# Two heads' last 64 queries in one score tile, in an attention and mixture-of-experts kernel

## The chip, the cores and the metric

The kernel runs on one core of a Trainium2 chip. The metric is the device time of one execution in microseconds (us); lower is better. A core has TensorE (PE; its weight loads are shown as PEld), VectorE (DVE), ScalarE (ACT), GpSimd (POOL), SyncE (SP, here only an issuer of DMAs) and 16 DMA engines. TensorE's clock is granted at one of two levels, 1.2 or 2.4 GHz; the profile gives the granted clock as a share of the higher.

## What is computed

Attention with a threshold, then a dense block, then a routed block. Inputs are float32; the essence of the reference:

```python
# q, k, v: [4, 8, 576, 64]: 4 batches, 8 heads, 576 queries, 64 values a head
scores = scale * q @ k.T
scores = where(scores >= max(scores) - tau, scores, -1e9)
attn = exp(scores - max) / (sum + 1e-9)
x = (attn @ v) as [2304, 512]
x = relu(x @ w_in) ** 2 @ w_out                  # 512 -> 2048 -> 512
# then: tokens with x @ w_skip > 0 go to one of 8 experts (argmax of x @ w_gate):
out = x + gate * (relu(x @ w1[e]) @ w2[e])       # 512 -> 1024 -> 512
```

## The kernel before

The 32 heads are worked on in 16 pairs g = 0, 2, ..., 30 (`pair`). The pairs 0 and 2 are computed in float32 (`pair32`, not changed). The other 14, the 16-bit pairs, split queries and keys into two float16 parts that lie side by side (buffer QK, the keys copied with their halves swapped into K2, named K in the profile), so that two matmuls give a float32-like score. The 576 queries of a head are 4 tiles of 128 and one of 64. `UNITS` groups them as (0, 1), (2, 3) and (4).

One tile is `tile_step`: scores on TensorE into a pair of PSUM banks (S, ps_s in the profile), row maximum and limits on VectorE, the exponential on ScalarE, the mask with the row sum (acc) on VectorE, the float16 high part on ScalarE, and the float16 residue on GpSimd, into a piece of hl. `transpose` then turns a unit (one or two tiles) by a DMA into et0, et1 or et2. `av` multiplies them with the values (v12) into the PSUM bank a, and its sum goes to xo: one `av` for the first 256 queries, one for the other 320. The tiles come in the order: five of head x = 0, five of head x = 1. `finish_pair` inverts the sums (rd), stores them to rd_d, and stores xo to xT_d.

The 2304 tokens are then worked on in nine blocks of 256 (`moe_block`). A block loads its tokens into xr and the stored inverse sums into rb (`ld_scale`), scales them, and splits them into xh and xl. Its 16 steps (`moe_step`) each multiply into a bank (ps_h; in late blocks also ps_t, ps_a), take r = ReLU, hh = r squared on ScalarE, r again as the exact square on VectorE, hlo = r - hh (GpSimd in blocks 0 to 4, VectorE later), and multiply by the second weights into ps_o. The weights of the dense block come in 64-bit form and are decoded by `decode` during attention; the last two units of each kind pass through xr, which no block can use meanwhile. The routed block (`second`) comes after block 8; its weights are loaded and cast from the end of block 8 on (L1484, L1488).

Nothing of the order is written out by hand. Every piece of work is a task of `Flow` with an engine, a cost, and the buffers that it uses; a list scheduler plans all of them, 20 times over, with each task's longest tail in the plan as its priority, and the best plan is issued. Each engine then works off its own list in order. A buffer kind has a count: one et0, et1 and et2, two QK, two K2, three e, two r, two hh, one hlo; three score buffers until pair 6, then two; two banks a until pair 6, then one.

Of the kernel before, what the change touches and what calls it, by code (L numbers as in the profile page):

```python
# [231 lines left out]
P = 128  # L232
# [4 lines left out]
def kernel(  # L237
# [120 lines left out]
    CH = 0  # L358
# [58 lines left out]
    def kind(name, n, gate=None):  # L417
# [22 lines left out]
        "pc": (6, [P, 5], F32),  # L440
        "QK": (2, [P, 2 * NQ, P], F16), "K2": (2, [P, S], F16),
        "e": (3, [P, S], F32),
        "et0": (1, [P, 2, NB, P], F16), "et1": (1, [P, 2, NB, P], F16), "et2": (1, [P, 1, NB, REM], F16),
        "xo": (1, [P, S], F32), "sm": (6, [P, 3], F32),
        "acc": (3, [P, 2, NQ], F32), "rd": (3, [P, 2, NQ], F32),
    }
    for n, (c, shape, dt) in ATT.items():
# [26 lines left out]
    flow.kind("etf", [tuple(chunks(i * NQ * P * 4, NQ * P * 4)) for i in range(NF)])  # L474

    MOE = {
        "r": (2, [P, BLK], F32), "hh": (2, [P, BLK], F32R),
        "hlo": (1, [P, BLK], F32R),
        "lg": (2, [P, TPB, E + 1], F32), "gs": (2, [P, 8, TPB], F32),
        "t1": (2, [P, TPB, E], F32), "t2": (2, [P, TPB, E], F32),  # L480
# [111 lines left out]
    def pair(g, parts):  # L592

        s0 = g * NQ
        f = lambda z: s0 - NQ + z
        nqk, nv, v12, vs, qs, pc, spl = (Buf(n) for n in ("nqk", "nv", "v12", "vs", "qs", "pc", "sp"))
        kl, ql = Buf(), Buf()
        queued(sp, "nqk", s0 - 2 * NQ + 1, 1100, lambda on: load_k(on, nqk.at, g), writes=[kl], alloc=[nqk], ns=1200, any=1)
        sp(s0 - 2 * NQ + 1.1, 600, lambda on: load_q(on, nqk.at, g), writes=[ql], alloc=[nqk], ns=1800, any=1)
        queued(sp, "nv", s0 - NQ - 1, 1100, lambda on: load_v(on, nv.at, g), writes=[nv], ns=1800, any=2)  # L600
        if g == AF:
            def clear():
                for j in (KB, NQ + KB):
                    nc.gpsimd.memset(nqk.at[REM:P, :, j, :], 0.0)

            pool(400, s0 - 2 * NQ + 1, clear, parts=[kl, ql], alloc=[nqk], after=[last["nqk"]])
        ready = split(g, f, nqk, kl, ql, qs, pc, spl)
        values(g, f, nv, v12, vs)
        qks = [keys(x, lambda z: f(z + x * NQ), spl, ready[x]) for x in range(2)]
        for units in parts:  # L610
            xo, acc, rd = (Buf(n) for n in ("xo", "acc", "rd"))
            t0, t1 = UNITS[units[0]][0], UNITS[units[-1]][1]
            for x in range(2):
                et = {}
                for u in units:
                    a, b = UNITS[u]
                    et[u] = Buf(f"et{u}")
                    hl = Buf("hl2" if b - a > 1 else "hl")
                    hs = [tile_step(s0 + i - t0, g, u, i, hl, *qks[x], pc, x, acc) for i in range(a, b)]
                    transpose(s0 + b - 1 - t0, u, hl, hs, et[u])  # L620
                    if u != 1:
                        us = range(max(0, u - 1), u + 1)
                        av(s0 + b - t0, g, x, us, [et[z] for z in us], v12, vs, xo)
                s0 += t1 - t0
            finish_pair(g, t0, t1, acc, rd, xo)

    def pair32(g):
# [43 lines left out]
    def tiles32(g, x, a, b, nv, qk, acc, rd, xq):  # L671
        ps2 = Buf("a0" if g < AE else "a")
        done = []
        for i in range(a, b):
            o, m = QT[i]
            s_ = g * NQ + x * NQ + i
            part = Buf()
            ps, e = tile_step(s_, g, 0, i, None, None, None, None, x, acc, qk, part)
            done.append(part)
            et = Buf("etf")  # L680
            fv = lambda ps=ps: ps.at.rearrange("p a b -> p (a b)")

            def turn(m=m, e=e, fv=fv):
                for t in range(NQ):
                    n = min(P, S - t * P)
                    nc.tensor.transpose(
                        fv()[0:n, t * P:t * P + m], e.at[:m, t * P:t * P + n], idf[0:m, 0:m])

            def move(m=m, et=et, fv=fv):
                for r, t0, t1 in ((P, 0, KB), (REM, KB, NQ)):  # L690
                    nc.scalar.copy(
                        out=et.at[0:r, t0:t1, 0:m],
                        in_=fv()[0:r, 0:NQ * P].rearrange("p (t q) -> p t q", q=P)[:, t0:t1, 0:m])

            def product(m=m, et=et, c=(i - a) * D):
                for t in range(NQ):
                    n = min(P, S - t * P)
                    nc.tensor.matmul(  # L698
                        out=ps2.at[:m, c:c + D], lhsT=et.at[0:n, t, 0:m], rhs=nv.at[0:n, x, t, :],
                        start=t == 0, stop=t == NQ - 1)  # L700

            pe(690 if m == P else 380, s_ + 0.4, turn, reads=[e], writes=[ps], heat=0.5)
            queued(act, "hl", 650, CH + s_ + 0.5, move, reads=[ps], writes=[et])
            queued(pe, "av", AV, s_ + 0.6, product, reads=[et, nv], writes=[ps2], heat=0.5)

        def inverse():
            nc.vector.tensor_scalar(
                out=rd.at[:, x, a:b], in0=acc.at[:, x, a:b], scalar1=1e-9 * ESC, scalar2=None, op0=ALU.add
            )
            nc.vector.reciprocal(out=rd.at[:, x, a:b], in_=rd.at[:, x, a:b])  # L710

        k = min(b, KB)

        def scaled():
            nc.vector.tensor_tensor(
                out=xq.at[:, a:k, x], in0=ps2.at[:, 0:(k - a) * D].rearrange("p (t d) -> p t d", d=D),
                in1=rd.at[:, x, a:k, None].to_broadcast([P, k - a, D]), op=ALU.mult)

        def rest_():
            nc.scalar.activation(  # L720
                out=xq.at[0:REM, KB, x], in_=ps2.at[0:REM, (KB - a) * D:(NQ - a) * D],
                func=ACTF.Copy, scale=rd.at[0:REM, x, KB:NQ])

        r = Buf()
        dve(300, -20, inverse, reads=[acc] + done, writes=[r], alloc=[rd], port=1)
        dve(150 + 68 * (k - a), -20, scaled, reads=[ps2, r], parts=[xq], alloc=[rd])
        if b > KB:
            act(190, -20, rest_, reads=[ps2, r], parts=[xq], alloc=[rd])
# [131 lines left out]
        for z in range(a, b):  # L860
            stores.setdefault(bb * NQ + z, []).extend(ts)

    def tile_step(s, g, u, i, hl, QK, K2, pc, x, acc, qk32=None, done=None):
        o, m = QT[i]
        ps, e, sm = Buf("S3" if g < SE else "S"), Buf("e0" if g < EE else "e"), Buf("sm")
        h = Buf()
        row = i - UNITS[u][0]
# [12 lines left out]
                    out=fv()[:m, c], lhsT=qk32.at[0][r, o:o + m], rhs=qk32.at[1][r, c], start=True, stop=True)  # L880

        def scores():
            qk = QK.at.rearrange("p t d -> p (t d)")
            for c in (slice(0, KB * P), slice(KB * P, S)):
                for src, k0 in ((qk, NQ * P), (K2.at, 0)):
                    nc.tensor.matmul(  # L886
                        out=fv()[:m, c], lhsT=qk[:, o:o + m],
                        rhs=src[:, k0 + c.start:k0 + c.stop], start=k0 > 0, stop=k0 == 0,
                    )

        top = lambda: fv()[:m, S:S + 1]

# [31 lines left out]
        if qk32:  # L924
            queued(pe, "S", 1220, s, scores32, reads=[qk32], writes=[ps], heat=0.5)
        else:
            queued(pe, "S", 530, s, scores, reads=[QK, K2], writes=[ps])
        dve(670, CB + s + 0.1, rowmax, reads=[ps], writes=[sm])
        dve(314, CB + s + 0.11, limits, reads=pcs + [ps], writes=[sm])
        act(718, CB + s + 0.2, expo, reads=pcs + [ps, sm], writes=[e])  # L930
# [4 lines left out]
        pool(1382, CH + s + 0.5, lo, reads=[e], writes=[h], alloc=[hl])  # L935
        return h

    def transpose(s, u, hl, hs, et):
        n = len(hs)
        m = QT[UNITS[u][0]][1]  # L940

        def dma(_):
            nc.sync.dma_start_transpose(
                out=et.at.rearrange("p t n q -> p (t n) q"),
                in_=hl.at[:m].rearrange("p t n -> p (t n)"),
            )

        queued(sp, "et", CH + s + 0.6, 1500 * n if m == P else 750, dma, ns=None, reads=hs, writes=[et], alloc=[hl])

    def av(s, g, x, us, ets, v12, vs, xo):  # L950

        n = [sum(QT[i][1] for i in range(*UNITS[u])) for u in us]
        o = QT[UNITS[us[0]][0]][0]
        ps = Buf("a0" if g < AE else "a")
        top, low = (slice(z * D, z * D + D) for z in (x, 1 - x))

# [2 lines left out]

        def mm():  # L960
            c = 0
            for et, w in zip(ets, n):
                for z in range(NB):
                    vals = v12.at[:, x, z % NQ]
                    for a in range(2) if apart else (slice(0, 2),):
                        lhsT = vals[:, a] if apart else vals.rearrange("p a d -> p (a d)")
                        nc.tensor.matmul(  # L967
                            out=ps.at[0:D if apart else P, c:c + w], lhsT=lhsT, rhs=et.at[:, :, z, :],
                            start=z == 0 and a != 1, stop=z == NB - 1 and a != 0,
                        )  # L970
                c += w
# [107 lines left out]
    def moe_block(j):  # L1079
# [22 lines left out]
        for c in range(2):  # L1102
# [3 lines left out]
            y = j * BLK  # L1106
            while y < (j + 1) * BLK:
                bb, o = divmod(y, S)
                n = min(S - o, (j + 1) * BLK - y)
                ks = [z for z in range(2) if not wide_(bb * H + 4 * c + 2 * z)]  # L1110
                if ks:
                    if todo and todo[-1][0] == ks and todo[-1][2] == y - j * BLK:
# [11 lines left out]
            def ld_scale(on, c=c, rb=rb, todo=todo):  # L1124
                for ks, _, _, segs in todo:
                    for z in range(2):
                        for bb, o, n, w in segs:
                            h0 = 4 * c + 2 * ks[0] + z
                            on.dma_start(
                                out=rb.at[z * D:(z + 1) * D, ks[0]:ks[-1] + 1, w:w + n],  # L1130
                                in_=rd_d[bb, h0:h0 + 2 * len(ks) - 1:2, o:o + n][None].to_broadcast([D, len(ks), n]),
                            )
# [693 lines left out]
```

## Time and profile before

| what | value |
|---|---|
| runs | 1065.97 us (median of 3: 1063.48, 1065.97, 1066.58) |
| profiled execution | 1064.44 us, of it 1062.9 us from its first to its last instruction (the span) |
| busy share of the span | PE 84%, DVE 74%, ACT 57%, POOL 39% |
| mean granted clock of TensorE | 0.901 |
| chain of work that ended last, by engine | PE 55%, DVE 17%, DMA 12%, ACT 6% |

The busy shares are means over stages that differ: the 32-bit pairs, then 16-bit pairs alone, then 16-bit pairs with the blocks 0 to 4 between their tiles, then the rest of the blocks, then the routed block. An engine's share says little without its stage. In the rows, times are us unless marked ns, L886 is line 886 of the kernel before, and "128x1 f32<-128x576 f32" reads: 128 partitions by 1 element from 128 partitions by 576.

### The profile page before, as it was taken

To read this page: it belongs to the slowest core of one execution; us is meant where nothing else is said; L and a number is where in the kernel's file an instruction comes from. 1 tells how busy PE (TensorE), PEld (TensorE's weight loads), DVE (VectorE), ACT (ScalarE), POOL (GpSimd) and SP (SyncE) were. 2 spreads that over 40 slices of the span, in tenths; PEclk is the share of its full clock that TensorE was granted. 3 is DMA by queue.
4 is the path that set the end of the run, shared out by engine and by line. 5 is a ranking of instruction groups with operands and counts; after the bars stand their busy time and mean duration, and the time that the engine had idled before them with its cause. 6 is when DMAs were issued, how large, how long until landed. Compare 5 with 4: busy or idle time off the path is not lost.

```text
span 1062.9 us, 16377 instructions
## 1 busy us (share of the span) xinstructions
PE 890.8 (84%) x5272; PEld 706.9 (67%) x5272; DVE 791.5 (74%) x1927; ACT 602.7 (57%) x1033; POOL 416.1 (39%) x546
## 2 busy tenths in 40 slices
PE   6999843527997899897789798999999996889895
PEld 3676621316775786676666677889999975677674
DVE  6999799869886989995898884445454775688771
ACT  5678676757765777674665764212121552757761
POOL 2323356546565677574565763401010011121211
PEclk9995565659998999898899998999999997989998
DMA  6434586999989999899968998612010536778850
GB/s 172 142 108 142 141 181 123 152 148 175 133 163 103 128 187 200 182 118 126 157 150 162 104 154 81 196 41 80 1 41 1 163 119 238 275 269 293 303 208 21
DMA packets 293864, 156.14 MB, mean 147 GB/s; under 512 B 240468, under 2 KB 266580, under 8 KB 293776
## 3 DMA queue, kind: packets, MB, share of 16 engines
q1 hardware_dynamic: 290096, 148.19, 67.0%
q0 software_dynamic: 3680, 6.89, 2.2%
q8 instruction: 42, 0.69, 0.3%
q14 instruction: 46, 0.38, 0.1%
HBM read 89.29 MB, written 17.28 MB: 100 GB/s over the span
## 4 chain that ended last, share of the span: by engine, by line
PE 55%; DVE 17%; DMA 12%; ACT 6%; issue 4%; SPq 3%; POOL 2%; DVEq 0%; ACTq 0%; POOLq 0%
PE ps_h L1166 9%; PE ps_t L1166 6%; PE ps_o L1176 4%; PE ps_o L1178 4%; PE ps_o L1177 4%; PE ps_o L1588 4%; PE ps_s L879 3%; PE ps_a L967 3%; DVE e L909 3%; PE ps_s L886 3%; DVE ps_s L894 3%; DMA K<-QK 3%; PE ps_t L1556 3%; PE ps_h L698 2%; DMA et<-hl 2%
## 5 line engine op out<-in xcount | busy, mean ns | idle before, releaser
L919 POOL TENSOR_TENSOR hl<-e,hl 128x64 f16<-128x64 f32 (+2 forms) x276 | 205.5, 771 | 122.8 <-ACT hl L915 106.3
L1166 PE MATMUL ps_h<-xh,w 128*128 128x256 f32 x720 | 144.6, 298 | 13.0 <-DVE r L1198 8.1
L886 PE MATMUL ps_s<-QK 128*128 128x512 f16 (+1 forms) x280 | 88.9, 322 | 71.3 <-DVE e L909 70.0
L886 PEld LDWEIGHTS <-QK 128*128 128x128 f16 (+1 forms) x560 | 52.6, 109 | 141.3 <-issue 106.3
L906 ACT ACTIVATE e<-ps_s,sm,pc 128x576 f32<-128x576 f32 (+1 forms) x138 | 112.6, 827 | 50.1 <-DVE sm L901 42.3
L1196 ACT ACTIVATE hh<-r 128x256 fp32r<-128x256 f32 x144 | 60.1, 417 | 141.1 <-DVE r L1191 99.5
L909 DVE SCALAR_TENSOR_TENSOR e<-ps_s,sm,e 128x576 f32<-128x576 f32 (+1 forms) x153 | 122.5, 806 | 17.5 <-ACT e L906 16.6
L894 DVE TENSOR_REDUCE ps_s<-ps_s 128x1 f32<-128x576 f32 (+1 forms) x160 | 120.0, 755 | 19.7 <-PE ps_s L886 15.4
L1166 PEld LDWEIGHTS ps_h<-xh,w 128*128 128x128 f32 x720 | 116.7, 197 | 23.9 <-DVE r L1198 15.1
L1176 PE MATMUL ps_o<-w,hh 128*128 128x512 f32 x288 | 120.5, 418 | 0.0
L915 ACT CAST hl<-e 128x576 f16<-128x576 f32 (+1 forms) x138 | 91.9, 669 | 47.3 <-DVE e L909 31.6
L1178 PE MATMUL ps_o<-w,hlo 128*128 128x512 f32 x288 | 114.9, 399 | 3.4 <-DVE hlo L1202 2.2
L1177 PE MATMUL ps_o<-w,hh 128*128 128x512 f32 x288 | 114.4, 397 | 0.0
L1166 PE MATMUL ps_h<-xl,w 128*128 128x256 f32 x360 | 103.6, 288 | 0.5 <-POOL xl L1147 0.4
L1202 POOL TENSOR_TENSOR hlo<-r,hh 128x256 fp32r<-128x256 f32 x80 | 64.3, 804 | 79.8 <-DVE r L1198 39.2
L1488 DVE TENSOR_TENSOR w<-stg,w 128x1024 fp32r<-128x1024 f32 x63 | 75.7, 1220 | 21.5 <-ACT w L1484 20.8
L967 PE MATMUL ps_a<-et,v 128*128 128x256 f16 (+1 forms) x738 | 78.3, 262 | 12.6 <-DVE xo L980 8.6
L1484 ACT CAST w<-stg 128x1024 fp32r<-128x1024 f32 x63 | 65.0, 1049 | 25.8 <-PE ps_o L1588 11.0
L967 PEld LDWEIGHTS <-v 128*128 128x128 f16 x756 | 60.8, 104 | 28.4 <-issue 10.4
L886 PE MATMUL ps_s<-K,QK 128*128 128x512 f16 (+1 forms) x280 | 71.0, 321 | 4.2 <-DMA K<-QK 4.2
L1041 POOL TENSOR_TENSOR w<-tmp,w 128x512 fp32r<-128x512 f32 x28 | 38.8, 1393 | 83.7 <-ACT tmp L1038 69.1
L1166 PEld LDWEIGHTS ps_h<-xl,w 128*128 128x128 f32 x360 | 70.6, 196 | 0.9 <-POOL xl L1147 0.9
(286 smaller groups left out, 2036.7 us busy)
## 6 DMA issues: line engine op xcount, KB each, us to landing
stg<-in_moe_w_dram SPq DMA_DIRECT2D x63, 512.0 KB, 5.2
raw<-in_moe_w_in_dram SPq DMA_DIRECT2D x14, 512.0 KB, 4.4
raw<-in_moe_w_out_dram SPq DMA_DIRECT2D x14, 512.0 KB, 3.6
big<-in_moe_w_dram SPq DMA_DIRECT2D x13, 512.0 KB, 5.2
xr<-in_moe_w_dram SPq DMA_DIRECT2D x12, 512.0 KB, 5.0
xT_d<-xo SPq DMA_DIRECT2D x16, 288.0 KB, 4.7
xr<-xT_d SPq DMA_DIRECT2D x9, 512.0 KB, 4.6
x_d<-big SPq DMA_DIRECT2D x18, 256.0 KB, 4.5
```

Source lines behind the costliest of these rows:

```text
L886: nc.tensor.matmul(out=fv()[:m, c], lhsT=qk[:, o:o + m], rhs=src[:, k0 + c.start:k0 + c.stop], start=k0 > 0, stop=k0 == 0,)
L894: nc.vector.tensor_reduce(out=top(), in_=sv(), axis=AX.X, op=ALU.max)
L906: nc.scalar.activation(out=ev(), in_=sv(), func=ACTF.Exp, bias=col(1), scale=pc.at[:m, 0:1])
L909: nc.vector.scalar_tensor_tensor(out=ev(), in0=sv(), scalar=col(2), in1=ev(), op0=ALU.is_ge, op1=ALU.mult, accum_out=acc.at[:m, x, i:i + 1],)
L915: nc.scalar.copy(out=hl.at[:m, row, 0:S], in_=e.at[:m])
L919: nc.gpsimd.tensor_tensor(out=hl.at[:m, row, w:w + n], in0=e.at[:m, c:c + n], in1=hl.at[:m, row, c:c + n], op=ALU.subtract,)
L967: nc.tensor.matmul(out=ps.at[0:D if apart else P, c:c + w], lhsT=lhsT, rhs=et.at[:, :, z, :], start=z == 0 and a != 1, stop=z == NB - 1 an ...
L1166: nc.tensor.matmul(out=ps.at[:, 0:BLK], lhsT=a[:, kk, :], rhs=b[:, kk, :], start=kk == z == 0, stop=kk == KC - 1 and z == 2,)
L1176: nc.tensor.matmul(out=p, lhsT=hh.at[:, sl], rhs=bh, start=m == 0, stop=False)
L1177: nc.tensor.matmul(out=p, lhsT=hh.at[:, sl], rhs=bl, start=False, stop=False)
L1178: nc.tensor.matmul(out=p, lhsT=hl.at[:, sl], rhs=bh, start=False, stop=m == KF - 1)
L1488: nc.vector if on == "DVE" else nc.gpsimd).tensor_tensor(
```

## The change

The last 64 queries of both heads of a 16-bit pair are put into one tile of 128 rows: the first head's on partitions 0 to 63, the second's on 64 to 127. It is the fifth of the pair's now nine tiles, between four of the first head and four of the second. Its row sums stand in one column of acc, and the two heads' parts are told apart where the inverse sums are read back. et2 has 128 columns where it had 64, and r has one buffer where it had two. The last two changed pieces below belong to `moe_block`: blocks are read in pieces that end at query 512 of a batch, and the pieces behind it are read from the shared column.

```diff
-        "et0": (1, [P, 2, NB, P], F16), "et1": (1, [P, 2, NB, P], F16), "et2": (1, [P, 1, NB, REM], F16),
+        "et0": (1, [P, 2, NB, P], F16), "et1": (1, [P, 2, NB, P], F16), "et2": (1, [P, 1, NB, P], F16),
...
-        "r": (2, [P, BLK], F32), "hh": (2, [P, BLK], F32R),
+        "r": (1, [P, BLK], F32), "hh": (2, [P, BLK], F32R),
...
+            both = Buf("et2")
             for x in range(2):
-                et = {}
-                for u in units:
+                et = []
+                for u in range(2):
                     a, b = UNITS[u]
-                    et[u] = Buf(f"et{u}")
-                    hl = Buf("hl2" if b - a > 1 else "hl")
-                    hs = [tile_step(s0 + i - t0, g, u, i, hl, *qks[x], pc, x, acc) for i in range(a, b)]
-                    transpose(s0 + b - 1 - t0, u, hl, hs, et[u])
-                    if u != 1:
-                        us = range(max(0, u - 1), u + 1)
-                        av(s0 + b - t0, g, x, us, [et[z] for z in us], v12, vs, xo)
-                s0 += t1 - t0
+                    et.append(Buf(f"et{u}"))
+                    hl = Buf("hl2")
+                    hs = [tile_step(s0 + i, g, u, i, hl, [qks[x]], pc, x, acc) for i in range(a, b)]
+                    transpose(s0 + b - 1, hl, hs, et[u])
+                    if not u:
+                        av(s0 + b, g, x, 0, et, None, v12, vs, xo)
+                s0 += KB
+                if not x:
+                    hl = Buf("hl")
+                    hs = [tile_step(s0, g, 2, KB, hl, qks, pc, 0, acc)]
+                    transpose(s0, hl, hs, both)
+                av(s0 + 1 - x, g, x, 1, et, both, v12, vs, xo)
+                s0 += 1 - x
...
         def scores():
+            for z, (QK, K2) in enumerate(qks):
+                qk = QK.at.rearrange("p t d -> p (t d)")
+                for c in (slice(0, KB * P), slice(KB * P, S)):
+                    for src, k0 in ((qk, NQ * P), (K2.at, 0)):
+                        nc.tensor.matmul(
+                            out=fv()[z * w:z * w + w, c], lhsT=qk[:, o:o + w],
+                            rhs=src[:, k0 + c.start:k0 + c.stop], start=k0 > 0, stop=k0 == 0,
+                        )
...
     def ld_scale (moe_block):
-                n = min(S - o, (j + 1) * BLK - y)
+                n = min((KB * P if o < KB * P else S) - o, (j + 1) * BLK - y)
...
                             h0 = 4 * c + 2 * ks[0] + z
+                            if o >= KB * P:
+                                h0, o = h0 - z, o + z * REM
```

`av` now takes its last 64 columns from the part of et2 that is its head's. The plan is made anew, so rows move on every engine; three places follow, with the buffers' numbers as the program gives them.

TensorE, from the fourth tile of the first head on, in pair 4, where 16-bit work begins (QK_188 and K_193 are the first head's, QK_189 and K_194 the second's; the weight loads between are left out). Before:

```order
L886 MATMUL ps_s_144<-K_193,QK_188 128x64
...
L886 MATMUL ps_s_148<-QK_188 64x512
...
L886 MATMUL ps_s_148<-K_193,QK_188 64x512
...
L886 MATMUL ps_s_148<-QK_188 64x64
...
L886 MATMUL ps_s_148<-K_193,QK_188 64x64
...
L886 MATMUL ps_s_140<-QK_189 128x512
```

Now:

```order
L897 MATMUL ps_s_144<-K_193,QK_188 128x64
...
L897 MATMUL ps_s_140<-QK_188 64x512
...
L897 MATMUL ps_s_140<-K_193,QK_188 64x512
...
L897 MATMUL ps_s_140<-K_193,QK_188 64x64
...
L897 MATMUL ps_s_140<-QK_189 64x512
...
L897 MATMUL ps_s_140<-K_194,QK_189 64x512
...
L897 MATMUL ps_s_140<-K_194,QK_189 64x64
...
L897 MATMUL ps_s_148<-QK_189 128x512
```

The second head's keys are read one tile sooner, into the same score buffer as the first head's last queries.

VectorE, where the first step of block 0 (r_253) stands among the tiles of the 16-bit pairs (ps_s is a row maximum, sm the limits, e the mask, xo an output; xr_249 by big is the block's scaling). Before, at row 443 of VectorE's list and on:

```order
L901 TENSOR_SCALAR sm_224<-ps_s_140,pc_182 128x1
L909 SCALAR_TENSOR_TENSOR e_200,acc_231<-ps_s_144,sm_223,e_200 128x576
L909 SCALAR_TENSOR_TENSOR e_198,acc_231<-ps_s_140,sm_224,e_198 128x576
L583 CAST qs_174<-qs_174 128x2
L894 TENSOR_REDUCE ps_s_144<-ps_s_144 128x1
L1198 SCALAR_TENSOR_TENSOR r_253<-ps_h_136,r_253 128x256
L894 TENSOR_REDUCE ps_s_140<-ps_s_140 64x1
```

Now, at row 412 and on:

```order
L920 SCALAR_TENSOR_TENSOR e_199,acc_230<-ps_s_144,sm_223,e_199 128x576
L920 SCALAR_TENSOR_TENSOR e_198,acc_230<-ps_s_140,sm_224,e_198 128x576
L1205 TENSOR_SCALAR r_253<-ps_h_136 128x256
L849 TENSOR_SCALAR acc_230<-acc_230 128x10
L861 RECIPROCAL rd_236<-acc_230 128x10
L1212 SCALAR_TENSOR_TENSOR r_253<-ps_h_136,r_253 128x256
L905 TENSOR_REDUCE ps_s_144<-ps_s_144 128x1
```

The step stood at row 448, after 54 row maxima of the whole kernel; it now stands at row 417, after 47.

SP's queue, around the load of block 0's tokens (xr_249 from xT_d) and the decode's loads into the same buffer (from in_moe_w_in and in_moe_w_out). Before:

```order
L1012 DMA xr_249<-in_moe_w_in_dram 128x4x256
L943 DMA_TRANSPOSE et_208<-hl 128x18x128
L943 DMA_TRANSPOSE et_212<-hl 128x9x64
L849 DMA rd_d<-rd_237 128x10x1
L849 DMA rd_d<-rd_235 128x10x1
...
L1012 DMA xr_249<-in_moe_w_out_dram 128x1024
...
L1093 DMA xr_249<-xT_d 128x4x256
L1129 DMA big<-rd_d 64x2x256 x2
```

Now:

```order
L1024 DMA xr_249<-in_moe_w_in_dram 128x4x256
L855 DMA rd_d<-rd_237 128x10x1
L855 DMA rd_d<-rd_235 128x10x1
...
L1105 DMA xr_249<-xT_d 128x4x256
L1143 DMA big<-rd_d 64x2x256 x2
...
L953 DMA_TRANSPOSE et_212<-hl 128x9x128
...
L1024 DMA xr_249<-in_moe_w_out_dram 128x1024
```

The fourth of the decode's loads through xr stood ahead of the block's tokens and now stands behind them.

## Rows read from the trace of the kernel before

**Rows 1.** Windows by stage: us, busy time (x instructions) per engine, granted clock, DMA.

```profile
core 0: us, PE busy (x) PEld busy (x) DVE busy (x) ACT busy (x) POOL busy (x), PEclk, DMA share, GB/s
...
120.00:250.00 130.00, 58.53 (x319) 33.87 (x318) 111.54 (x267) 87.92 (x139) 70.15 (x87) 0.62 0.84 147
250.00:660.00 410.00, 360.83 (x2480) 285.20 (x2481) 337.86 (x952) 269.87 (x496) 251.16 (x344) 0.95 0.95 144
660.00:850.00 190.00, 187.90 (x1240) 168.59 (x1239) 97.45 (x257) 47.08 (x107) 24.66 (x35) 1.00 0.26 74
```

**Rows 2.** Lines by form, a tile's chain: busy us, mean ns, idle before.

```profile
L894 DVE TENSOR_REDUCE ps_s<-ps_s 128x1 f32<-128x576 f32 x128 | 96.1, 756 | 15.9 <-PE ps_s L886 12.4 <-PE ps_s L879 2.7
...
L919 POOL TENSOR_TENSOR hl<-e,hl 64x512 f16<-64x512 f32 x28 | 33.1, 1182 | 0.0
...
L909 DVE SCALAR_TENSOR_TENSOR e<-ps_s,sm,e 64x576 f32<-64x576 f32 x31 | 24.9, 804 | 4.2 <-ACT e L906 4.0
...
L894 DVE TENSOR_REDUCE ps_s<-ps_s 64x1 f32<-64x576 f32 x32 | 24.0, 751 | 3.8 <-PE ps_s L886 3.0 <-issue 0.3
...
L906 ACT ACTIVATE e<-ps_s,sm,pc 64x576 f32<-64x576 f32 x28 | 23.0, 822 | 10.2 <-DVE sm L901 9.5 <-POOL hl L919 0.5
...
L915 ACT CAST hl<-e 64x576 f16<-64x576 f32 x28 | 18.7, 666 | 6.1 <-DVE e L909 5.8
...
L897 DVE TENSOR_SCALAR sm<-ps_s,pc 64x1 f32<-64x1 f32 x28 | 7.3, 262 | 0.2
...
L901 DVE TENSOR_SCALAR sm<-ps_s,pc 64x1 f32<-64x1 f32 x28 | 5.6, 199 | 0.0
```

**Rows 3.** TensorE's waits, 250 to 660 us: us in total, times, longest.

```profile
PE ps_s L886 <- DVE e L909: 9.6, 11, 3.0
...
PE ps_s L886 <- DMA K<-QK: 4.2, 3, 2.9
```

**Rows 4.** Lines by form, a score matmul of a whole and of a 64-query tile.

```profile
L886 PE MATMUL ps_s<-QK 128*128 128x512 f16 x112 | 48.6, 434 | 54.3 <-DVE e L909 53.2 <-ACT xo L745 0.6
...
L886 PE MATMUL ps_s<-QK 128*64 128x512 f16 x28 | 12.6, 448 | 17.0 <-DVE e L909 16.8
```

**Rows 5.** Timeline of DVE, SP and PE, 226 to 245 us: start, us.

```profile
226.99 0.49 DVE L1015 TENSOR_SCALAR big<-xr 128x512 int32<-128x512 int32 x1 [7.41 <-DMA xr<-in_moe_w_out_dram]
...
234.94 0.37 SPq L1093 DMA_DIRECT2D xr<-xT_d  x1
...
244.08 0.48 PE L1166 MATMUL ps_h<-xh,w 128*128 128x256 f32 x2
```

**Rows 6.** Timeline around r: third stage, mixed stage, a cast in block 8.

```profile
753.18 0.42 DVE L1191 TENSOR_SCALAR r<-ps_h 128x256 f32<-128x256 f32 x1 [0.90 <-PE ps_h L1166]
...
754.69 0.42 DVE L1202 TENSOR_TENSOR hlo<-r,hh 128x256 fp32r<-128x256 f32 x1
756.00 0.42 DVE L1191 TENSOR_SCALAR r<-ps_a 128x256 f32<-128x256 f32 x1 [0.89 <-PE ps_a L1166]
...
411.57 0.37 ACT L1189 ACTIVATE r<-ps_h 128x256 f32<-128x256 f32 x1
412.16 1.31 POOL L1202 TENSOR_TENSOR hlo<-r,hh 128x256 fp32r<-128x256 f32 x1
...
847.53 1.21 DVE L1488 TENSOR_TENSOR w<-stg,w 128x1024 fp32r<-128x1024 f32 x1
```

**Rows 7.** Timeline of SP and PE, 548 to 557 us, pair 26.

```profile
548.17 1.18 SPq L763 DMA_DIRECT2D K<-QK  x2
...
552.13 0.40 PE L886 MATMUL ps_s<-QK 128*64 128x512 f16 x1
...
552.62 0.20 PE L886 MATMUL ps_s<-K,QK 128*64 128x64 f16 x1
556.20 0.38 PE L886 MATMUL ps_s<-QK 128*128 128x512 f16 x1 [0.36 <-DVE e L909]
```

**Rows 8.** DMA issues: count, KB each, median us to landing.

```profile
K<-QK SPq DMA_DIRECT2D x14, 72.0 KB, 4.3
...
oT<-rd_d SPq DMA_DIRECT2D x4, 32.0 KB, 3.6
```

More of the change, by code (lines that the diff above doesn't have):

```diff
@@ L677, in tiles32 @@
             part = Buf()
-            ps, e = tile_step(s_, g, 0, i, None, None, None, None, x, acc, qk, part)
+            ps, e = tile_step(s_, g, 0, i, None, None, None, x, acc, qk, part)
             done.append(part)
@@ L861, in finish_pair, with tile_step @@
             stores.setdefault(bb * NQ + z, []).extend(ts)
-    def tile_step(s, g, u, i, hl, QK, K2, pc, x, acc, qk32=None, done=None):
+    def tile_step(s, g, u, i, hl, qks, pc, x, acc, qk32=None, done=None):
         o, m = QT[i]
+        w = m
+        if not qk32:
+            m = P
         ps, e, sm = Buf("S3" if g < SE else "S"), Buf("e0" if g < EE else "e"), Buf("sm")
@@ L882, in scores @@
         def scores():
[L883 to L889, printed above, removed]
+            for z, (QK, K2) in enumerate(qks):
[6 more added lines that the diff above has]
+                        )
         top = lambda: fv()[:m, S:S + 1]
@@ L926, in tile_step @@
         else:
-            queued(pe, "S", 530, s, scores, reads=[QK, K2], writes=[ps])
+            queued(pe, "S", 530 * len(qks), s, scores, reads=[z for qk in qks for z in qk], writes=[ps])
         dve(670, CB + s + 0.1, rowmax, reads=[ps], writes=[sm])
@@ L936, in tile_step, with transpose @@
         return h
-    def transpose(s, u, hl, hs, et):
+    def transpose(s, hl, hs, et):
         n = len(hs)
-        m = QT[UNITS[u][0]][1]
         def dma(_):
@@ L944, in dma, with av @@
                 out=et.at.rearrange("p t n q -> p (t n) q"),
-                in_=hl.at[:m].rearrange("p t n -> p (t n)"),
+                in_=hl.at.rearrange("p t n -> p (t n)"),
             )
[L948 to L953, printed above, removed]
+        queued(sp, "et", CH + s + 0.6, 1500 * n, dma, ns=None, reads=hs, writes=[et], alloc=[hl])
+    def av(s, g, x, u, ets, both, v12, vs, xo):
+        n = [2 * P] + [REM] * (both is not None)
+        o = u * 2 * P
+        cuts = [(ets[u], slice(0, P))] + ([(both, slice(x * REM, x * REM + REM))] if both else [])
+        ets = [z for z, _ in cuts]
         ps = Buf("a0" if g < AE else "a")
@@ L961, in mm @@
             c = 0
-            for et, w in zip(ets, n):
+            for (et, q), w in zip(cuts, n):
                 for z in range(NB):
@@ L967, in mm @@
                         nc.tensor.matmul(
-                            out=ps.at[0:D if apart else P, c:c + w], lhsT=lhsT, rhs=et.at[:, :, z, :],
+                            out=ps.at[0:D if apart else P, c:c + w], lhsT=lhsT, rhs=et.at[:, :, z, q],
                             start=z == 0 and a != 1, stop=z == NB - 1 and a != 0,
```

## The prediction

> **What bounds the kernel now.** I read the share of busy time by stage first [rows 1]. There are four stages behind the 32-bit pairs (0 to 120 us, untouched by the change). From 120 to 250 us three 16-bit pairs run while the weights are decoded, and no mixture-of-experts block has begun: VectorE is busy 111.5 of 130 us, TensorE 58.5, at a granted clock of 0.62. From 250 to 660 us the other eleven pairs run with blocks 0 to 4 between them: TensorE 360.8 of 410 us, VectorE 337.9, ScalarE 269.9, GpSimd 251.2. From 660 to 850 us TensorE alone counts, 187.9 of 190 us. The last stage has nothing of the change in it. So the first of these stages is set by VectorE, the second mostly by TensorE with VectorE close behind, the third by TensorE. TensorE's work stays what it is, so the end moves by what TensorE's idle time (71.5 us, then 49.2 us) gains or loses.
>
> Then I looked at one tile by its forms [rows 2]. What the reader is to see: a tile of 64 queries costs as much as one of 128, since time goes by the 576 columns. The row maximum takes 751 ns on 64 partitions and 756 ns on 128. Last come the waits of TensorE in the mixed stage [rows 3]: the longest is 9.6 us in all, for a score bank that the mask (L909) still holds. TensorE's idle time there has many small causes.
>
> **The change, part by part.** *Tiles merged.* Each of 14 pairs has nine elementwise chains where it had ten. A chain of the 64-query form is, on VectorE, 751 + 262 + 199 + 804 = 2016 ns; on ScalarE 822 + 666 = 1488 ns; on GpSimd 1182 ns for the long half of the residue and a short second part [rows 2]. Over 14 pairs that is 28.2 us of VectorE and 20.8 us of ScalarE. Two transposing DMAs become one of twice the rows; their bytes are the same.
>
> *TensorE.* The shared tile has the same eight matmuls as two 64-query tiles, and the value products have the same count and widths. A half's first matmul takes 448 ns against 434 ns for a full one [rows 4]; I count nothing.
>
> *The stage to 250 us.* The order shows 448 VectorE rows ahead of the first block's r in the kernel before and 417 now. Seven tiles' maxima, limits and masks are no longer ahead of it (three have gone, four now come after it), and the decode of the last weight unit through xr has also moved behind it. Seven chains are 7 x 2.016 = 14.1 us; VectorE is busy 86% of this stage, so 12 us. The block's first matmul stands at 244.08 us, right after its input is loaded into xr (234.94 us), which waited for that fourth decode, and the decode for its load (VectorE idle 7.41 us) [rows 5]. So two causes let the block start earlier; I take 12 us, not their sum, because the load into xr also waits for the slow store of the pair's sums. TensorE is idle 55% of this stage, so 12 us more of it with work is 12 x 0.55 = 6.6 us gained. Bounds: nothing, if xr's load stays as late; 14 us, if TensorE takes up all of it.
>
> *The mixed stage.* Eleven chains are 22.2 us of VectorE's 337.9 (6.6%) and 16.4 of ScalarE's 269.9 (6.1%). If TensorE's 49.2 us of idle time fell in the same share, that would be 3.2 us; if VectorE were the only limit, 22.2 us. The stage is nearer to the first, with TensorE 88% busy, but some of its time runs at a low clock (0.95 in the mean) and comes back with denser work: I take 5 us. Bounds 0 and 22.2.
>
> *One buffer r instead of two.* Now a step's ReLU may start before the subtraction of the step before it has read r; afterwards it can't. In the third stage it already doesn't: one subtraction starts at 754.69 us and lasts 0.42 us, the next ReLU starts at 756.00 [rows 6], 0.89 us of slack in a step of 2.82 us (the distance of two ReLUs there). In the mixed stage there are steps in which it does: a ReLU at 411.57 us, while the earlier step's subtraction on GpSimd runs from 412.16 for 1.31 us [rows 6]. That step would begin 1.9 us later, and the bank of its matmul would come free as much later. At the end of the third stage the casts of the next weights, 1.21 us each [rows 6], stand between the steps on VectorE: ReLU, square, product and subtraction are some 1.9 us with their handoffs, 3.1 us with a cast, against 2.82 us. Sixteen steps of 0.3 us are 5 us. I take a loss of 2 us for all of it; bounds 0 and 12.
>
> *The second head's keys are wanted a tile sooner.* The shared tile stands fifth and multiplies by both heads' keys; the second head's first tile stood sixth. In pair 26 the copy of the keys is issued at 548.17 us, such copies land 4.3 us later (median) [rows 8], so at about 552.5 us; the fifth tile starts at 552.13, the sixth at 556.20 [rows 7]. A slack of 3.7 us becomes a wait of 0.4 us. TensorE takes its rows in order, so block steps and value products behind those scores wait too. The buffers of the first head likewise come free at the fifth tile and are wanted again four tiles later, not five. I take a loss of 1 us; bounds 0 and 14 (1 us a pair).
>
> *The scales.* The rows of 1/sum are now read by 12 more DMAs of 32 KB, in blocks 4, 6 and 8. Such a one lands in 3.6 us [rows 8]. Blocks 6 and 8 lie in the stage where TensorE has 160 us of queued work, so they are covered; for block 4 the cover is the steps of block 3. Nothing, and at worst one landing, 3.6 us.
>
> The sum: -6.6 - 5 + 2 + 1 = -8.6 us, on the profiled execution's 1064.44 us (its span is 1062.9): 1055.8, so 1056 us. That execution lies 1.5 us under the median of the runs shown, 1065.97, which is less than what the terms leave open.
>
> **A rule weighed against the rows.** A score matmul on half the array takes as long as a full one [rows 4], one after the other, and the sum counts it so. The Trainium skill's page TensorEngine Tiling (Array Packing), Tiling Modes, says that the array's tiles work independently and that different ones can load weights and multiply in parallel; the shared tile's two halves write different partitions, so by that rule they could overlap. No row of before has two such halves in a row. Half of the shared tile's matmuls would then vanish: a 64-query tile's four took some 0.7 us (552.13 to 552.82 us [rows 7]), and 14 of them are 9.8 us of TensorE, which would put the end at 1046. I give it 4 in 100.
>
> **The rivals.** *Slower: the single r.* If in the mixed stage a quarter of the 80 steps lose 1 us on TensorE's path (20 us), and the end of the third stage loses 5, the sum is -11.6 + 1 + 25: 1079 us. It decides from 0.14 us a step on 80 steps, where the 11.6 us of gains are gone. For it: the GpSimd subtraction that lasts 1.31 us, behind chains of residues of 1.18 us. Against it: only some ReLUs lead, and the slack in the third stage. 12 in 100. *Slower: the keys.* With 2 us a pair lost (28 us) and r's 2 us, 1064.4 - 11.6 + 30 = 1083; at 1 us a pair it is 1069, the edge. For it: TensorE already waited for such copies in the mixed stage, 4.2 us in all [rows 3]; against: the planner can fill the space with block steps. 8 in 100. *No change:* the block's start stays tied to the store of sums and xr's load, and the mixed stage to TensorE: gains of 1 to 4, losses of as much, 1062 to 1067. 14 in 100. *Much faster:* the mixed stage follows VectorE (22.2) and the start brings 14: 1064.4 - 36 + 3 = 1031; between it and my forecast, say 1040. 10 in 100.
>
> **How the numbers follow.** My forecast (1047 to 1062) has the remaining 52 in 100. About 0.3% of the median, 3.2 us, is what a measurement can tell from no change. Faster: 0.52 + 0.10 + 0.04 = 0.66. Same: 0.14. Slower: 0.20. The range leaves out a tenth at either end: 1040, where the case much faster begins, to 1072, past the edge of the keys' case.
>
> **What would show it.** Right: 140 row maxima of 16-bit pairs become 126, all on 128 partitions; the first block's matmul stands near 232 us; TensorE's idle time up to 660 us falls by some 9 us; the stage of TensorE alone keeps its 2.82 us a step. Wrong: ReLUs that wait for the subtraction of the step before, TensorE rows of the shared tile that wait for the copy of keys, a block start that is still near 244 us, or an attention that ends earlier while its TensorE work is only pushed into the third stage.

## The result, and the profile after

The changed kernel takes 1049.55 us (median of 4 runs, 1047.54 to 1054.27) where the kernel before took 1064.72 beside it on the same chip: 0.987 of it, 95% interval 0.982 to 0.991. On another chip, later, it took 1057.84 (9 runs) against 1067.24: 0.992 [0.990, 0.995]. The profiled execution took 1047.54 us, its span 1046.0. Times are medians of all executions; ratios, here and below, are of means, without the few executions that lie over 1.5% above the fastest of their kernel.

The stages of [rows 1] now, in the columns of those rows:

```profile
120.00:250.00 130.00, 68.50 (x397) 44.46 (x397) 108.04 (x266) 84.95 (x138) 66.81 (x82) 0.71 0.82 159
250.00:660.00 410.00, 356.25 (x2494) 280.67 (x2490) 318.48 (x901) 254.34 (x473) 236.79 (x328) 0.96 0.95 147
660.00:850.00 190.00, 188.87 (x1250) 171.32 (x1249) 104.89 (x266) 48.51 (x105) 23.12 (x32) 1.00 0.25 80
```

In the stage to 250 us TensorE has 10 us more work than before (block 0 starts earlier); from 250 to 660 us it has 4.6 us less and VectorE 19.4 us less. TensorE's idle time in the two stages is 61.5 + 53.8 = 115.3 us, before 120.6. But the stages are cut at fixed times, and the work in them has moved; the accounts below use the whole span.

The chain of a tile, and the score matmuls of a half tile, by form, as in [rows 2] and [rows 4]:

```profile
L920 DVE SCALAR_TENSOR_TENSOR e<-ps_s,sm,e 128x576 f32<-128x576 f32 x134 | 106.5, 810 | 9.4 <-ACT e L917 7.4 <-issue 1.0
L905 DVE TENSOR_REDUCE ps_s<-ps_s 128x1 f32<-128x576 f32 x142 | 105.8, 757 | 21.9 <-PE ps_s L897 15.3 <-PE ps_s L889 5.8
...
L897 PE MATMUL ps_s<-K,QK 128*64 128x512 f16 x28 | 7.0, 435 | 3.8 <-DMA K<-QK 3.8
L897 PE MATMUL ps_s<-QK 128*64 128x512 f16 x28 | 6.5, 441 | 8.4 <-DVE e L920 8.4
```

142 row maxima on 128 partitions are the 16 of the 32-bit pairs and the 126 that were forecast. In the last two rows the reader is to see the two numbers behind the bar: 28 matmuls of 441 ns are busy for 6.5 us only. Before, 28 of 448 ns were busy for 12.6 us [rows 4]. Busy time counts a moment once: now nearly every pair of them lies in the same moment. TensorE's timeline around the shared tile of one pair shows it (start, us; "x2" is two matmuls in one row):

```profile
473.45 0.18 PE L584 MATMUL ps_a<-vs,ones 128*128 128x1 bf16 x1
473.56 0.42 PE L897 MATMUL ps_s<-QK 128*64 128x512 f16 x2
473.80 0.39 PE L897 MATMUL ps_s<-K,QK 128*64 128x512 f16 x2
474.01 0.21 PE L897 MATMUL ps_s<-QK 128*64 128x64 f16 x2
474.04 0.21 PE L897 MATMUL ps_s<-K,QK 128*64 128x64 f16 x2
474.19 0.18 PE L584 MATMUL ps_a<-qs,ones 128*128 128x2 bf16 x1
```

All eight matmuls of the shared tile end 0.69 us after the first begins, the time of the four of a half tile before (552.13 to 552.82 us [rows 7]), and other work of TensorE starts at 474.19. In the program the second head's four stand behind the first head's four.

The load of block 0's tokens, its scaling and the first block matmul, from the timeline [rows 5]:

```profile
225.75 0.51 SPq L1105 DMA_DIRECT2D xr<-xT_d  x1
...
232.19 1.64 DVE L1153 TENSOR_TENSOR xr<-xr,big 128x512 f32<-128x512 f32 x1
...
234.08 0.78 PE L1180 MATMUL ps_h<-xh,w 128*128 128x256 f32 x2
```

TensorE's waits from 250 to 660 us, as in [rows 3]:

```profile
PE ps_h L1180 <- DVE r L1212: 11.0, 16, 2.4
PE ps_s L897 <- DVE e L920: 7.5, 13, 1.7
PE ps_o L1192 <- POOL hlo L1216: 7.0, 4, 3.3
...
PE ps_s L897 <- DMA K<-QK: 5.4, 2, 3.8
```

The wait for the mask has fallen from 9.6 to 7.5 us, the wait for the keys has grown from 4.2 to 5.4, and the longest in all is now one for a step of the blocks (the product r, 11.0 us; 7.9 before). The step of the third stage is what it was: 2.82 us between two ReLUs, the subtraction done well before [rows 6]:

```profile
753.30 0.42 DVE L1205 TENSOR_SCALAR r<-ps_t 128x256 f32<-128x256 f32 x1 [0.90 <-PE ps_t L1180]
...
754.80 0.43 DVE L1216 TENSOR_TENSOR hlo<-r,hh 128x256 fp32r<-128x256 f32 x1
756.12 0.42 DVE L1205 TENSOR_SCALAR r<-ps_t 128x256 f32<-128x256 f32 x1 [0.90 <-PE ps_t L1180]
```

### The profile page after: what moved, and what is told of

Same layout as the page of the kernel before. It is cut to its first block, busy times and chain, and to the rows that moved or that the text cites. A ratio compares the mean times of both kernels' runs of the same rounds, so it can differ in the third digit from the quotient of the medians.

```text
span 1046.0 us, 16199 instructions
## 1 busy us (share of the span) xinstructions
PE 883.7 (84%) x5272; PEld 701.3 (67%) x5272; DVE 763.7 (73%) x1866; ACT 580.0 (55%) x996; POOL 395.4 (38%) x516
## 4 chain that ended last, share of the span: by engine, by line
PE 33%; DVE 14%; issue 13%; DMA 10%; ACT 5%; POOL 4%; SPq 2%; DVEq 0%; POOLq 0%; ACTq 0%
PE ps_h L1180 7%; PE ps_t L1180 5%; PE ps_o L1192 4%; PE ps_o L1190 3%; DMA QK<-sp 3%; PE ps_o L1191 3%; DVE e L920 3%; DVE ps_s L905 3%; PE ps_a L979 3%; PE ps_s L897 2%; PE ps_o L1602 2%; DVE sp L833 1%; POOL hl L930 1%; DMA K<-QK 1%; DVE r L1212 1%
## 5 line engine op out<-in xcount | busy, mean ns | idle before, releaser
L930 POOL TENSOR_TENSOR hl<-e,hl 128x64 f16<-128x64 f32 x246 | 184.7, 778 | 98.5 <-ACT hl L926 94.8
L1192 PE MATMUL ps_o<-w,hlo 128*128 128x512 f32 x288 | 115.3, 400 | 11.3 <-POOL hlo L1216 7.4
L905 DVE TENSOR_REDUCE ps_s<-ps_s 128x1 f32<-128x576 f32 (+1 forms) x146 | 108.8, 756 | 21.9 <-PE ps_s L897 15.3
L917 ACT ACTIVATE e<-ps_s,sm,pc 128x576 f32<-128x576 f32 x123 | 98.8, 827 | 40.4 <-DVE sm L912 33.3
L920 DVE SCALAR_TENSOR_TENSOR e<-ps_s,sm,e 128x576 f32<-128x576 f32 (+1 forms) x138 | 109.7, 809 | 9.5 <-ACT e L917 7.4
L897 PEld LDWEIGHTS <-QK 128*128 128x128 f16 (+1 forms) x560 | 46.4, 107 | 100.8 <-issue 67.1
L897 PE MATMUL ps_s<-QK 128*128 128x64 f16 (+2 forms) x280 | 77.1, 316 | 35.6 <-DVE e L920 31.2
L926 ACT CAST hl<-e 128x576 f16<-128x576 f32 x123 | 80.5, 667 | 23.9 <-DVE e L920 21.0
L1216 POOL TENSOR_TENSOR hlo<-r,hh 128x256 fp32r<-128x256 f32 x80 | 60.8, 760 | 78.0 <-DVE r L1212 52.5
L1192 PEld LDWEIGHTS ps_o<-w,hlo 128*128 128x128 f32 x288 | 54.7, 190 | 30.0 <-POOL hlo L1216 11.7
```

The source lines that it names most:

```text
L897: nc.tensor.matmul(out=fv()[z * w:z * w + w, c], lhsT=qk[:, o:o + w], rhs=src[:, k0 + c.start:k0 + c.stop], start=k0 > 0, stop=k0 == 0,)
L905: nc.vector.tensor_reduce(out=top(), in_=sv(), axis=AX.X, op=ALU.max)
L917: nc.scalar.activation(out=ev(), in_=sv(), func=ACTF.Exp, bias=col(1), scale=pc.at[:m, 0:1])
L920: nc.vector.scalar_tensor_tensor(out=ev(), in0=sv(), scalar=col(2), in1=ev(), op0=ALU.is_ge, op1=ALU.mult, accum_out=acc.at[:m, x, i:i + 1],)
L926: nc.scalar.copy(out=hl.at[:m, row, 0:S], in_=e.at[:m])
L930: nc.gpsimd.tensor_tensor(out=hl.at[:m, row, w:w + n], in0=e.at[:m, c:c + n], in1=hl.at[:m, row, c:c + n], op=ALU.subtract,)
```

## The experiments

Three explanations stood at the start: block 0 begins earlier; VectorE has 14 chains fewer; and the plan, made anew, happens to be better or worse, whatever the change. Each ratio is to the kernel before in runs beside it.

**Parts of the change.** *One buffer r alone:* the kernel before with `"r": (1, ...)`.

> The kernel before with one buffer r instead of two, nothing else (the plan is made anew). If one buffer costs what the prediction took, +2 us (0.2%); if it costs nothing, within 0.3% of the kernel before; if part of the measured gain is the new plan's luck, a move of 5 us or more either way. A ReLU that waits for the subtraction of the step before would show as idle time of TensorE before the next block matmul.

Measured: 1074.04 us, 1.011 [1.007, 1.014]. Its first block matmul stands at 230.75 us, earlier than in the change, and the kernel is slower than before. An early block 0 is thus not enough.

*The order without the shared tile,* with one r:

```diff
-                    hs = [tile_step(s0, g, 2, KB, hl, qks, pc, 0, acc)]
-                    transpose(s0, hl, hs, both)
+                    for z in range(2):
+                        hl = Buf("hl")
+                        hs = [tile_step(s0 + z, g, 2, KB, hl, [qks[z]], pc, z, acc)]
+                        transpose(s0 + z, hl, hs, each[z], REM)
```

> The new order without the merging: two tiles of 64 queries stand side by side in the place of the shared tile, each with its own chain of maximum, exponential, mask and casts and its own transposing DMA. One buffer r. If the removed chains are the gain, it is gone: within 0.5% of the kernel before, or slower by up to 10 us since the second head's keys are wanted a tile sooner with nothing saved. If the order itself (output products and buffers) were the gain, -8 us or more.

Measured: 1086.65 us, 1.023 [1.020, 1.027]. It is the slowest of all, though nothing in it is wider or longer than in before_r1 (et2 has two buffers of 64 columns there); the change itself, with the tiles in the same place but merged, is 3 to 4% faster. That difference holds three things at once: the chains, the shared matmuls and the plan. Its TensorE waits for copies of the keys before score matmuls are 1.6 us in all, so its loss isn't the keys; its first block matmul stands at 268.66 us, 24.6 us later than in the kernel before. Its timeline of TensorE holds the best comparison for the shared tile, the same eight matmuls, but with both halves on rows 0 to 63 of two banks:

```profile
347.96 0.40 PE L900 MATMUL ps_s<-QK 128*64 128x512 f16 x1
348.20 0.38 PE L900 MATMUL ps_s<-K,QK 128*64 128x512 f16 x1
348.42 0.19 PE L900 MATMUL ps_s<-QK 128*64 128x64 f16 x1
348.45 0.20 PE L900 MATMUL ps_s<-K,QK 128*64 128x64 f16 x1
348.48 0.38 PE L900 MATMUL ps_s<-QK 128*64 128x512 f16 x1
348.70 0.38 PE L900 MATMUL ps_s<-K,QK 128*64 128x512 f16 x1
348.91 0.19 PE L900 MATMUL ps_s<-QK 128*64 128x64 f16 x1
348.94 0.20 PE L900 MATMUL ps_s<-K,QK 128*64 128x64 f16 x1
```

One after the other: 347.96 to 349.14, that is 1.18 us against 0.69 in the shared tile.

*The shared tile in some pairs only* (one r): `JOIN = lambda g: g < 12` for the first four 16-bit pairs, `g >= 12` for the last ten; the others as before.

> Shared tile in the pairs 4 to 10 alone (10 is the pair in which block 0 begins); the pairs 12 to 30 keep two 64-query tiles. One buffer r. Theory A (the gain is made before block 0 and carried to the end): most of the 15 us, some -11 to -15 us. Theory B (each merged pair gives the same, about 1.1 us): 4/14 of it, -4 us.

> Shared tile in the pairs 12 to 30 alone; the pairs 4 to 10 keep two 64-query tiles. One buffer r. Theory A: 0 to -3 us, as in the stretch with blocks, which got 2.3 us shorter. Theory B: 10/14 of the gain, -11 us.

Measured: 1061.99 us, 1.001 [0.998, 1.004], and 1072.65 us, 1.011 [1.008, 1.014]. Ten of 14 merged pairs are slower than four. No gain by pair explains that (theory A isn't borne out either: -11 to -15 us were expected of the four); it made the plan the suspect.

**The plan's own scatter.** In before and in the change, the cost by which the planner counts a mask is 736 instead of 730. The work is the same, the order is another.

```diff
-        dve(730, CB + s + 0.3, mask, ...
+        dve(736, CB + s + 0.3, mask, ...
```

> The kernel before, with the planner told that a mask takes 736 ns and not 730; the same instructions, in another plan. If a plan made anew moves the time little, within 0.3%; if the gain of 15 us can be a plan's luck, a move of 5 us or more.

> The changed kernel with the same nudge of the planner. In this plan all four decodes through xr stand before block 0, whose first r stands at VectorE's row 435 (417 in the change, 448 before). If the gain is the removed work, -12 to -17 us against the kernel before. If it is the early start of block 0 that this one plan found, some -5 us.

Measured: before 1066.09 us, 0.999 [0.995, 1.002]; the change 1064.27 us, 0.997 [0.993, 1.000]. The same change in another order takes 0.4 to 1.0% longer than the change's own order (0.992 and 0.987 on two chips).

**The start of block 0.** In the change, block 0's load is put behind the whole decode (`if j <= 1` for `if j == 1`); in before, the decode's last load through xr is put behind block 0's load.

> The changed kernel with one dependency more: block 0's tokens are loaded into xr only behind the whole decode, as they stood in the kernel before. Theory of the start (block 0 ahead of the fourth decode is what gave the 10 us): -3 to -8 us against the kernel before, block 0 near 244 us. Theory of the removed work: -12 us or more.

> The kernel before with block 0's tokens loaded into xr ahead of the last decode, as in the change, and no tile merged. Theory of the start: -5 to -10 us, block 0 near 234 us. Theory of the removed work: within 0.3%, since VectorE has as much to do ahead of the block (first r at row 446 against 448).

Measured: 1073.59 us, 1.006 [1.003, 1.009], and 1081.47 us, 1.012 [1.007, 1.018]. In the first, the order at xr is the one that was asked for (the fourth decode's load at 213.99 us, the tokens' at 228.18; in the change 247.12 and 225.75), but it didn't delay the block: the new plan decodes sooner, the first block matmul stands at 234.66 us as in the change (234.08), and the kernel is 1.4 to 1.9% slower than the change, whose ratios are 0.992 and 0.987. In the second it moved 3.4 us ahead (240.67), and the kernel is slower. Over all these kernels (the table below has every start) the time doesn't follow this start where it lies between 223 and 245 us. order_only, slowest and latest with 268.66 us, may have lost by its delay; no run tells.

**The single r again, and more plans.** `r1_order_r2` is before_r1 in exactly its order, but the steps take two r in turn. `r1_nudge` is before_r1, and `after_nudge2` the change, with a mask cost of 736 and 724; `after_again` is the change.

```diff
+        rt = place["r"][len(turns) % 2]
...
-                nc.scalar.activation(out=r.at, in_=ps.at[:, 0:BLK], func=ACTF.Relu)
+                nc.scalar.activation(out=rt, in_=ps.at[:, 0:BLK], func=ACTF.Relu)
```

> The kernel before with one r (before_r1, 1.011 of before) in exactly its order of instructions, but each step's r now lies in the other of two buffers, so that a ReLU need not wait for the subtraction of the step before it. Nothing else differs from before_r1. Theory that the waits for the one r cost the time: the 11 us come back, 0.995 to 1.002 of before, and the TensorE waits whose other end is r (12.9 us by the dense block's first matmul between 250 and 650 us) shrink. Rival, that the order which the planner makes with one r costs it: 1.008 to 1.013 still, about 1074 us on a chip where before takes 1063. Half and half: 1.004 to 1.007.

> before_r1 (two r become one, tiles not merged) with the planner's cost of a mask 736 instead of 730, so another plan of the same work. If one r costs 1 percent by itself: 1.007 to 1.015 of before. If before_r1 was an unlucky plan: 0.998 to 1.005. With it, after and its two other plans have as many plans of the unmerged kernel beside them.

> The change itself on the chip of these runs, so that its other plans can be read beside it: 0.983 to 0.991 of before if what was measured first belongs to the kernel and not to the chip; nearer to 0.995 if the first measurement flattered it.

> The change with the planner's cost of a mask 724 instead of 730: another plan of the same work. The nudge to 736 gave 0.9965 of before, the change itself 0.987. If the change's worth lies near the middle of its plans: 0.987 to 0.997. If the change's own plan is the typical one and the nudge to 736 an unlucky one: 0.984 to 0.990. If the change's own plan is a lucky one: 0.994 to 1.000.

Measured, in that order: 1078.61 us, 1.009 [1.006, 1.013]; 1064.15 us, 0.998 [0.994, 1.001]; 1057.84 us, 0.992 [0.990, 0.995]; 1060.52 us, 0.994 [0.991, 0.996]. With two r in before_r1's order the 11 us don't come back, though 18 of its 144 ReLUs now start before the subtraction of the step before has ended (none in before_r1, 46 in the kernel before). So the waits for the one r weren't its loss. The waits of TensorE at 250 to 660 us on VectorE's product, in before_r1 and then with two r, are named "r" but are waits for the bank that this product (L1198, now L1201) reads:

```profile
PE ps_h L1166 <- DVE r L1198: 12.9, 12, 3.3
```

```profile
PE ps_h L1169 <- DVE r L1201: 13.8, 9, 5.2
```

And another plan with one r is as fast as before. The 1% of before_r1 was its order.

**The account.** TensorE's busy time over the whole span (windows), the part of it in the score matmuls of the 16-bit pairs, the span less the busy time, and the first block matmul (all in us):

| kernel (mask cost) | ratio | span | TensorE busy | of it scores | idle | VectorE busy | block 0 at |
|---|---|---|---|---|---|---|---|
| before (730) | 1 | 1062.9 | 890.8 | 106.6 | 172.1 | 791.5 | 244.1 |
| before_nudge (736) | 0.999 | 1065.9 | 890.8 | 106.6 | 175.1 | 796.9 | 245.0 |
| before_r1 (730) | 1.011 | 1075.2 | 891.9 | 100.9 | 183.3 | 796.8 | 230.8 |
| r1_nudge (736) | 0.998 | 1064.6 | 892.2 | 104.5 | 172.4 | 780.5 | 229.6 |
| the change (730) | 0.987 | 1046.0 | 883.7 | 91.5 | 162.3 | 763.7 | 234.1 |
| after_again (730) | 0.992 | 1054.1 | 883.5 | 92.6 | 170.6 | 766.8 | 234.8 |
| after_nudge (736) | 0.997 | 1058.1 | 875.4 | 91.7 | 182.7 | 763.5 | 223.4 |
| after_nudge2 (724) | 0.994 | 1061.7 | 880.6 | 94.0 | 181.1 | 771.6 | 242.3 |
| r1_order_r2, no shared tile | 1.009 | 1078.4 | 890.5 | 101.7 | 188.0 | 793.9 | 231.9 |
| block0_early, no shared tile | 1.012 | 1077.9 | 899.5 | 106.8 | 178.4 | 791.7 | 240.7 |
| order_only, no shared tile | 1.023 | 1087.9 | 908.6 | 106.6 | 179.3 | 801.0 | 268.7 |
| join_first4, in 4 pairs | 1.001 | 1060.2 | 898.8 | 105.0 | 161.4 | 783.7 | 230.8 |
| join_last10, in 10 pairs | 1.011 | 1069.0 | 884.1 | 96.0 | 184.9 | 766.7 | 236.3 |
| block0_late, in all pairs | 1.006 | 1073.0 | 880.6 | 93.4 | 192.4 | 760.8 | 234.7 |

Each row is one profiled execution. They come from several chips, on which the kernel before takes 1061 to 1068 us, so a difference of a few us between two rows says little.

The rows of before and of the change behind it (PE, PEld, DVE, ACT, POOL, clock):

```profile
0.00:1062.90 1062.90, 890.79 (x5272) 706.94 (x5272) 791.51 (x1927) 602.74 (x1033) 416.13 (x546) 0.90 0.70 147
```

```profile
0.00:1046.00 1046.00, 883.73 (x5272) 701.26 (x5272) 763.69 (x1866) 579.97 (x996) 395.39 (x516) 0.94 0.69 149
```

The same windows for the line of the score matmuls alone (L886, now L897; PE, PEld, clock):

```profile
0.00:1062.90 1062.90, 106.63 (x560) 52.59 (x560) 0.90 0.70 147
```

```profile
0.00:1046.00 1046.00, 91.52 (x560) 46.36 (x560) 0.94 0.69 149
```

*The time.* The first eight rows of the table are plans without the shared tile (two r or one) and with it, under no further constraint. The four without the shared tile lie between 0.998 and 1.011 (mean 1.002), the three with it between 0.987 and 0.997 (mean 0.993, the change taken at the mean of its two ratios): 0.9% or some 9 us. The two kinds don't mix, but their nearest plans (0.998 and 0.997) can't be told apart. By the scatter of so few plans the 9 us are uncertain by about as much (an estimate), and block0_late, merged in all pairs, is slower than the kernel before.

*TensorE's work.* Its busy time is 891.4 us in the mean of the four plans without the shared tile and 879.9 us in that of the three with it, 11.5 us less. The scores account for it: 104.7 and 92.6 us, 12.1 less, while all other work of TensorE stays (786.8 and 787.3 in the mean; 784 to 802 over the table). This fall doesn't hang on the plan: with the tile shared in all pairs the scores are busy 91.5 to 94.0 us, without it 100.9 to 106.8, whether the kernel is faster than before or slower.

*TensorE's idle time* is 175.7 and 176.8 us in the same means. So the fall in TensorE's work is as large as the gain, and no fall of its idle time is seen. But the idle time lies anywhere between 161 and 192 us over the table, as the plan falls, and a few us more or less of it, by the change, wouldn't show. By its idle time join_first4 is faster than join_last10, and block0_late slower than the kernel before, though their TensorE work says the opposite. The change's own plan is the best of its three: its idle time is 10 to 20 us under that of the other two.

## Why the prediction was right in its time and wrong about TensorE's work

1056 us was forecast, faster with 0.66. The time is 1049.55 us there and 1057.84 on the other chip: gains of 15.2 and 9.4 us where 8.6 were forecast. Most of the signs came too: 126 row maxima, a first block matmul near 232 us (234.08), 2.82 us a step in the third stage; TensorE's idle time in the two stages up to 660 us fell by 5.3 us, not by some 9. But the sum reached the time by terms that the runs don't bear out.

*TensorE, "I count nothing": this step failed.* Its work has fallen by 7.1 us in the profiled pair of kernels and by 11.5 us in the mean of the plans, where the scores account for all of it. The trace shows how: the two halves of the shared tile run beside each other, 0.69 us for 1.18. The Trainium skill's page TensorEngine Tiling (Array Packing), Tiling Modes, says that different tiles of the array can load weights and multiply in parallel; this trace agrees. From the rows: in three pairs, before 250 us, where the granted clock is 0.71 in the mean, the shared tile's first two matmuls together take 0.58 to 0.65 us where they take 0.42 later; there the difference is taken as double. 11 x 0.49 + 3 x 0.98 = 8.3 us, an estimate against 7.1 to 11.5 measured. It was the rival with 4 in 100, priced at 9.8 us and 1046. The rows weighed against the rule [rows 4] had each half tile alone; they could not speak against an overlap.

*Tiles merged, 28.2 us of VectorE: right as a price, but not as a gain.* VectorE's busy time fell by 27.8 us. From it 5 us less of TensorE's idle time in the mixed stage were forecast. From the first block matmul to the last 16-bit score (244.08 to 646.98 us before, 234.08 to 634.68 now) TensorE is idle 51.1 us before and 52.7 now: no gain there in this pair of kernels.

*The start, -6.6 us: the shift was right, its worth was not.* The first block matmul came 10 us earlier (12 forecast), and from the first 16-bit score to it (121.78 to 244.08 before, 126.85 to 234.08 now) TensorE is idle 60.9 us instead of 69.5. But before_r1 and r1_nudge begin block 0 at 230.75 and 229.6 us and take 1.011 and 0.998 of before; block0_late begins it at 234.66 and takes 1.006; after_nudge2, with the shared tile, begins it at 242.32, nearly as late as the kernel before, and takes 0.994. A shift of this size is not what sets the time.

*One r, +2 us: not told.* The third stage kept its step, two buffers in the same order (1.009 beside 1.011) bring nothing that can be told, and another plan with one r takes 0.998 [0.994, 1.001]. So the rival of a slower kernel by r, which needed some 25 us, is out; whether one r costs 0 or 2 us is below what these runs resolve.

*The keys, +1 us: right in the profiled pair of kernels.* The waits for K<-QK before score matmuls (L897) are 5.4 us in the mixed stage, 4.2 before. 3.8 us of them are one pair, in which the second half's matmuls had to wait for their keys at 393.63 us, after the first half's at 389.13. Over the whole span these waits are 5.5 to 7.3 us in the kernels with the shared tile in all pairs and 1.2 to 11.5 in those without, so the plan moves them by more than the change does. The two tiles side by side, which want the keys as soon, wait 1.6 us for them, so their 1.023 against before_r1's 1.011 isn't a price of the keys; two plans differ by as much.

*The scales, nothing:* no wait of TensorE on them stands among the rows of the mixed stage.

So the near hit owes something to luck. In the profiled pair of kernels TensorE's idle time did fall by 9.8 us (172.1 to 162.3), near the 8.6 of the sum, and its work by 7.1 us on top. In the mean of the plans the idle time doesn't fall and the work falls by 11.5 us: a gain near the forecast, but from the term that was counted as nothing. What more was measured on the first chip, 0.987 against the plans' 0.993, goes with this plan's low idle time. That the overlap, and not the shorter elementwise work, carries the gain is read from the accounts; no kernel ran that takes the overlap away alone and keeps the merged chains. That stays open.

## What to carry to other kernels

Where a tile of 64 is joined with another, look at which rows of the output each matmul writes: two groups on different halves can run beside each other on TensorE, and this saving comes on top of what VectorE and ScalarE save. Where a planner makes the order anew, a change of 1% in the time may be the order alone; run two or three plans of both kernels before a gain of 1% is put down to a cause. An earlier start of a stage, or less work on an engine beside the bound one, is a gain only if the bound engine's idle time over the whole span falls; look at that sum, and at the bound engine's own work, apart.

## What was not expected of the hardware

The second half's first matmul, fifth in TensorE's order, begins beside the first and so ahead of the second, third and fourth: one row of 0.42 us holds both, and one alone took 0.40 (at 347.96 us above). Where the second head's copied keys were late, that one matmul had run with the first half's, and the other three came over 4 us later:

```profile
389.13 0.42 PE L897 MATMUL ps_s<-QK 128*64 128x512 f16 x2
389.37 0.38 PE L897 MATMUL ps_s<-K,QK 128*64 128x512 f16 x1
...
393.63 0.40 PE L897 MATMUL ps_s<-K,QK 128*64 128x512 f16 x1 [3.82 <-DMA K<-QK]
```

And transfers that mostly land in 3 to 5 us (medians before: 3.6 us for QK<-sp, 3.4 and 4.3 for the copies of keys) sometimes take far longer, on the chain that ended last. Of the change (start, us):

```profile
320.00 19.56 DMA QK<-sp
374.17 11.31 DMA QK<-sp
```

In before there is, among others, a copy of keys at 317.55 us, 16.51 us long. Their cause wasn't looked for.
